# Taking weight loads out of the ends of the head groups of an attention-and-FFN backward kernel, and moving zero stores into them

## The chip, the cores and the metric

One core of one Trainium2 chip. The metric is the device time of one execution in microseconds (us), given as the median of the runs with the lowest and highest. "Span" is the same execution as the profiler sees it, some 1.8 us shorter than the time. "The median engine" of a store is the ninth of its sixteen landings.

## The reference

A decoder layer with attention over a window of a key-value cache and a gated FFN in parallel, forward and backward. Cut to what matters:

```python
# x 4x1x512; k_cache, v_cache 4x8x4096x128; wq 512x4096; wo 4096x512; FFN 512x1792; all bf16
def layer(x, k_cache, v_cache, wq, wo, w_gate, w_up, w_down):
    xn = layernorm(x)
    k, v = (repeat(c[:, :, 4096 - 1024:, :], 4, axis=1) for c in (k_cache, v_cache))   # the last 1024 of 4096
    o = softmax(q(xn @ wq) @ k.T / sqrt(128)) @ v
    return x + o @ wo + (gelu(xn @ w_gate) * (xn @ w_up)) @ w_down

out, vjp = jax.vjp(layer, ...)
return (out, *vjp(grad_out))          # the output and the gradients of x, both caches and all five weights
```

Two facts of it shape the kernel. The gradients of the two caches are as large as the caches (67 MB together), and three quarters of them are exact zeros, because only the last 1024 positions take part. Those zeros must still be written: 2 x 32 regions of 3072 x 128 bf16, 0.79 MB each, 50.3 MB of 112 MB moved in all.

## The kernel before

The eight key-value heads are worked through in NT = 4 groups of two heads (`GP = 2`). For each group the kernel loads slices of wo and wq (1 MB each) and blocks of both caches (`kb`, `vb`, 1 MB each), computes scores, softmax and its backward, and stores the gradients through staging buffers (`stg_dv`, `stg_dk`, `osb_o`, `osb_q`). SP issues these stores; GpSimd (POOL) issues the loads of the later groups; ACT issues the zero stores from one tile of zeros.

```python
    loads = deque()

    def load_w(t):
        eng = nc.gpsimd if t else nc.sync
        pool = wpool[t % 2]
        wo_t[t] = pool.tile([P, HG, D], BF16, name="wo_sb", tag="wo")
        eng.dma_start(out=wo_t[t][:], in_=wo_v[t])
        wq_t[t] = pool.tile([P, ND, CW], BF16, name="wq_sb", tag="wq")
        eng.dma_start(out=wq_t[t][:], in_=wq_v[t])
    ...
    def load_next(t):

        if t + 2 < NT:
            load_w(t + 2)
            for k in range(2):
                for g in range(GP):
                    loads.append(lambda k=k, g=g: load_kv(t + 2, k, g))
    ...
    def zeros(n):        # n regions, from one tile of zeros with ZP = 64 rows of 12 KB
        zs = ztile[0:P:P // ZP, :]
        while n > 0 and zruns:
            og, r = zruns[0]
            w = min(n, B * G - r, GP * 2)
            zsrc = bass.AP(tensor=zs.tensor, offset=zs.offset, ap=[list(zs.ap[0]), [0, w], [1, ZW]])
            zdst = og.rearrange("b g s d -> (b g) s d")[r:r + w, 0:K0, :].rearrange("r (m j) d -> m r (j d)", m=ZP)
            z = store(nc.scalar, zdst, zsrc, "zeros", ["rest", "zeros"])
            ...                     # ordered behind ACT's last evacuation
            n -= w
            ...
    def scores(t, k, hooks):        # k = 0 the keys, k = 1 the values
        for g in range(GP):
            for q in range(NQ):
                ...                 # transposes, evacuations and products of one K step
                if q == 1 and loads:
                    loads.popleft()()
                if q == 1:
                    zeros(ZN[t][GP * k + g])
    ...
        for t in range(NT):
            ...
            odq(t)
            fin(t)
            load_next(t)
            tick(len(bg))
            dw(t)
        tick(2)
        zeros(4)
        tick(len(bg))
        zeros(2 * B * G)            # whatever is left
```

Of the kernel before, what the change touches and what calls it, by code (L numbers as in the profile page):

```python
# [13 lines left out]
BF16 = mybir.dt.bfloat16  # L14
P = 128
# [3 lines left out]
def kernel(  # L19
# [29 lines left out]
    B, Sq, D = A_x.shape  # L49
# [7 lines left out]
    ND = D // P  # L57
# [4 lines left out]
    NT = G // GP  # L62
    HG = GP * rep
# [5 lines left out]
    CW = HG * Dh  # L69
# [46 lines left out]
    for c0 in range(0, NF, NF // 2):  # L116
        nc.sync.dma_start(out=wd_sb[:, c0:c0 + NF // 2, :],
                          in_=B_w_down[c0 * P:(c0 + NF // 2) * P, :].rearrange("(c p) n -> p c n", p=P))
# [47 lines left out]
    for b in range(B):  # L166
        nc.vector.tensor_copy(out=sel[:, :, b * rep:(b + 1) * rep],
                              in_=ident_f[:, b * RB:b * RB + 1].unsqueeze(2).broadcast_to([P, 2 * GP, rep]))
# [69 lines left out]
    for src, dstT, adj in ((dy_b, dyT, False), (xn_b, xnT, True)):  # L238
# [4 lines left out]
        if src is dy_b:  # L243
# [3 lines left out]
                                  in_=tps[:].rearrange("p c (b r) -> p c b r", b=B)[:, :, :, 0:8])  # L247
# [22 lines left out]
    wo_v = A_wo.rearrange("(t p k) n -> t p k n", p=P, k=HG)  # L270
    wq_v = A_wq.rearrange("(p c) (t j) -> t p c j", p=P, j=CW)
    wo_t, wq_t, k_t, v_t = {}, {}, {}, {}
# [3 lines left out]

    loads = deque()

    def load_w(t):
        eng = nc.gpsimd if t else nc.sync  # L280
        pool = wpool[t % 2]
        wo_t[t] = pool.tile([P, HG, D], BF16, name="wo_sb", tag="wo")
        eng.dma_start(out=wo_t[t][:], in_=wo_v[t])
        wq_t[t] = pool.tile([P, ND, CW], BF16, name="wq_sb", tag="wq")
        eng.dma_start(out=wq_t[t][:], in_=wq_v[t])

    def load_kv(t, k, g):
        d_, src, nm = ((k_t, A_k_cache, "kb"), (v_t, A_v_cache, "vb"))[k]
# [5 lines left out]
    def load_next(t):  # L294

        if t + 2 < NT:
            load_w(t + 2)
            for k in range(2):
                for g in range(GP):
                    loads.append(lambda k=k, g=g: load_kv(t + 2, k, g))  # L300
# [94 lines left out]
    def scores(t, k, hooks):  # L395

        lf = (qm, dom)[k]
        blks = (k_t, v_t)[k]
        ps = ps_a.tile([P, WQ], FP32, name="S_ps", tag=("S", "dP")[k])
        for g in range(GP):  # L400
            for q in range(NQ):
                T_ps = ps_w.tile([P, JQ, P], BF16, name="T_ps", tag="w")
                for jj in range(JQ):
                    nc.tensor.transpose(T_ps[:, jj, :], blks[(t, g)][:, q * JQ + jj, :], ident[:])  # L404
                T_sb = tsb.tile([P, WQ, B], BF16, name="T_sb", tag="T", bufs=4)
                evac(T_sb[:].rearrange("p n b -> p (n b)"), T_ps[:].rearrange("p j m -> p (j m)"), 1024, half=True)
                s = q * GP + g
                for b in range(B):
                    nc.tensor.matmul(ps[b * RG:(b + 1) * RG, :], lhsT=lf[:, b, s * RG:(s + 1) * RG],  # L409
                                     rhs=T_sb[:, :, b], start=(g == 0 and q == 0),  # L410
                                     stop=(g == GP - 1 and q == NQ - 1), tile_position=(0, b * RG))
                for f in hooks.get(g * NQ + q, ()):
                    f()
                tick(2 if k or q % 2 else 1)
                if q == 1 and loads:
                    loads.popleft()()
                if q == 1:
                    zeros(ZN[t][GP * k + g])
        st[t][("S", "dP")[k]] = ps[:]
# [90 lines left out]
    def odq(t):  # L510

        for j in range(J):
            for k in range(2):
                for g in range(GP):
                    pT, blks, r0 = st[t][("PT", "dST")[k]], (v_t, k_t)[k], (GP * k + g) * (P // 4)
                    nc.tensor.matmul(od_ps[r0:r0 + rep * B, 0, :], lhsT=pT[:, j % JQ, (j // JQ) * GP + g:P:NS],  # L516
                                     rhs=blks[(t, g)][:, j, :], start=(j == 0), stop=(j == J - 1),
                                     tile_position=(0, r0))
        rows = attw.tile([P, Dh], BF16, name="od_r", tag="od_r")
        nc.vector.tensor_scalar(out=rows[:], in0=od_ps[:, 0, :], scalar1=sc_od[:, 0:1], scalar2=None, op0=ALU.mult)  # L520
        T_ps = ps_w.tile([P, P], BF16, name="odT_ps", tag="w")
        nc.tensor.transpose(T_ps[:], rows[:], ident[:])
        dqT = attw.tile([P, GP, rep, B], BF16, name="od_T", tag="od_T")
        nc.vector.tensor_copy(out=dqT[:].rearrange("p g i b -> p g b i"),
                              in_=T_ps[:].rearrange("p (s x) -> p s x", s=2 * GP)[:, GP:2 * GP, 0:BI].rearrange(
                                  "p s (b i) -> p s b i", b=B))

        X = attw.tile([P, HG, Dh], BF16, name="od_x", tag="od_x", bufs=1)
        nc.gpsimd.tensor_tensor(out=X[:], in0=rows[:].unsqueeze(1).broadcast_to([P, HG, Dh]),
                                in1=hmsk[:].unsqueeze(2).broadcast_to([P, HG, Dh]), op=ALU.mult)  # L530
        st[t].update(dqT=dqT, X=X)
# [83 lines left out]


    NF4 = (NF + 3) // 4
    load_w(0)
    for k in range(2):
        for g in range(GP):  # L620
            load_kv(0, k, g)
# [141 lines left out]
    with tc.tile_pool(name="stage", bufs=4, reuse_waits="tile") as stage, \  # L763
            tc.tile_pool(name="wodd", bufs=1, reuse_waits="tile") as wodd:
        wpool.append(wodd)
        kvpool.append(wodd)
        load_w(1)
        for k in range(2):
            load_kv(1, k, 1)
        for t in range(NT):  # L770
            if t == 0:
                pre(t, {})
            masks(t)
            scores(t, 0, {})
            zeros(2 if t == 0 else 0)
            scores(t, 1, softmax(t))
            d1, d2 = softmax_d(t)
            zeros(4 if t == NT - 1 else 0)
            if t + 1 < NT:
                pre(t + 1, {0: [d1], 2: [d2]})  # L780
            else:
                tick(2)
                d1()
                tick(6)
                d2()
                tick(2)
            odq(t)
            fin(t)
            load_next(t)
            tick(len(bg))  # L790
            dw(t)
        tick(2)
        zeros(4)
        tick(len(bg))
        zeros(2 * B * G)


        acc_r = kvp.tile([P, 2, ND, B, RB], FP32, name="acc_r", tag="kb")
        nc.vector.tensor_copy(out=acc_r[:], in_=acc[:].unsqueeze(4).broadcast_to([P, 2, ND, B, RB]))
        fin_ps = []  # L800
        for o in range(2):
            f_ps = ps_w.tile([P, ND, P], FP32, name="f_ps", tag="w")
            for c in range(ND):
                nc.tensor.transpose(f_ps[:, c, :], acc_r[:, o, c].rearrange("p b r -> p (b r)"), ident_f[:])
            fin_ps.append(f_ps[:])
        acc_o, acc_d = fin_ps[0].rearrange("p c d -> p (c d)"), fin_ps[1].rearrange("p c d -> p d c")

        def adj(x):
            return x[:].rearrange("p (d c) -> p d c", c=ND)

        out_b = kvp.tile([P, D], BF16, name="out_b", tag="vb")
        nc.vector.tensor_tensor(out=out_b[:], in0=acc_o, in1=x_b[:], op=ALU.add)
        nc.sync.dma_start(out=out_0.rearrange("b s d -> (b s) d"), in_=out_b[0:P:RB, :])

        s1 = const.tile([P, 1], FP32, name="s1")
        nc.vector.reduce_sum(out=s1[:], in_=acc_d, axis=AX.XY)
        pr = kvp.tile([P, D], FP32, name="pr", tag="vb")
        s2 = const.tile([P, 1], FP32, name="s2")
        nc.vector.tensor_tensor_reduce(out=adj(pr), in0=acc_d, in1=adj(xn_f), scale=1.0, scalar=0.0,
                                       op0=ALU.mult, op1=ALU.add, accum_out=s2[:])  # L820
        nm1 = const.tile([P, 1], FP32, name="nm1")
        nc.vector.tensor_scalar(out=nm1[:], in0=s1[:], scalar1=-1.0 / D, scalar2=None, op0=ALU.mult)
        nm2 = const.tile([P, 1], FP32, name="nm2")
        nc.vector.tensor_scalar(out=nm2[:], in0=s2[:], scalar1=-1.0 / D, scalar2=None, op0=ALU.mult)
        nc.vector.scalar_tensor_tensor(out=adj(pr), in0=adj(xn_f), scalar=nm2[:, 0:1], in1=acc_d,
                                       op0=ALU.mult, op1=ALU.add)
        nc.vector.tensor_scalar(out=pr[:], in0=pr[:], scalar1=nm1[:, 0:1], scalar2=rstd[:, 0:1],
                                op0=ALU.add, op1=ALU.mult)
        dx_b = kvp.tile([P, D], BF16, name="dx_b", tag="kb")
        nc.vector.tensor_tensor(out=dx_b[:], in0=pr[:], in1=dy_b[:], op=ALU.add)  # L830
        nc.sync.dma_start(out=out_1.rearrange("b s d -> (b s) d"), in_=dx_b[0:P:RB, :])
# [30 lines left out]
```

## Time and profile before

| | before |
|---|---|
| time | 281.14 us (280.98 to 281.59, 3 runs) |
| span; mean granted TensorE clock | 279.9 us; 0.885 |
| PE, DVE, ACT, POOL busy | 77%, 57%, 41%, 20% |
| moved | 112.15 MB, 401 GB/s over the span |
| last compute | 269.1 us |
| last large store lands | 15 engines at 275.0 us, one at 278.8 us |

The last row is my reading of the semaphore updates in the trace: each large store has sixteen in this trace, and I take each as the landing of the part that one of the sixteen engines carries. The updates do not name the engines. The other rows are on the page. A page's slice view cuts the span into 40 equal slices, counted from 0 below. The stretch view gives a window, its length, then busy times with counts of instructions for PE, weight loads, DVE, ACT and POOL, then the clock, the mean busy share of the sixteen DMA engines, and GB/s.

### The profile page before, as it was taken

The numbers are of one execution on the slowest core, as the hardware profiler recorded it, in microseconds if no ns is written. First come the engines' busy times: TensorE is split into PE (matmuls) and PEld (weight loads), VectorE is DVE, ScalarE is ACT, GpSimd is POOL, SyncE is SP. The second block draws the span as 40 slices with busy tenths as digits, with TensorE's granted clock in tenths as the row PEclk, the third lists the DMA queues.
The fourth block names the chain that finished last, engine by engine and source line by source line (L and its number), as shares of the span: only waits on it lengthen the run. The fifth ranks groups of instructions, "written<-read, shape, count | busy, mean of one in ns | idle before, by whom it ended". The sixth has DMA issues, their size and how long they took to land.

```text
span 279.9 us, 7186 instructions
## 1 busy us (share of the span) xinstructions
PE 215.6 (77%) x3126; PEld 140.7 (50%) x3132; DVE 158.9 (57%) x336; ACT 115.3 (41%) x214; POOL 56.0 (20%) x56
## 2 busy tenths in 40 slices
PE   1868986978669869897799897778989769789700
PEld 0856864645346645454466654445665435255300
DVE  6955744645446655563657554547766444577740
ACT  1321733454335245543342553446245435714600
POOL 3890003230200334102001550010142020020000
PEclk9975979899986977997959979999999997898975
DMA  7999999999999999999999999999999999998992
GB/s 233 448 390 429 427 404 393 409 411 417 417 426 427 424 426 409 370 423 422 431 423 419 316 417 423 432 419 427 419 422 393 424 422 421 419 428 351 396 410 114
DMA packets 19440, 112.15 MB, mean 401 GB/s; under 512 B 1473, under 2 KB 5073, under 8 KB 10449
## 3 DMA queue, kind: packets, MB, share of 16 engines
q10 hardware_dynamic: 4416, 50.34, 42.8%
q1 hardware_dynamic: 12304, 44.58, 39.3%
q0 software_dynamic: 2688, 16.78, 15.4%
q8 instruction: 24, 0.39, 0.5%
q14 instruction: 8, 0.06, 0.1%
HBM read 30.68 MB, written 81.01 MB: 399 GB/s over the span
## 4 chain that ended last, share of the span: by engine, by line
PE 56%; DVE 21%; DMA 11%; issue 4%; ACT 2%; POOL 2%; ACTq 0%; DVEq 0%
PE kv_ps L544 11%; PE T_ps L404 9%; DVE T_sb L101 6%; PE S_ps L409 6%; DMA out_dram<-osb_d 6%; DMA out_dram<-osb_g 5%; PE dwo_ps L563 3%; PE acc_ps L213 3%; PE wgT_ps L749 3%; PE wqT_ps L602 3%; PE od_ps L516 3%; PE woT_ps L341 2%; POOL P_x L424 2%; PE pT_ps L435 2%; PE dwq_ps L575 2%
## 5 line engine op out<-in xcount | busy, mean ns | idle before, releaser
L101 DVE COPY T_sb<-T_ps 128x1024 bf16<-128x1024 bf16 x64 | 43.9, 690 | 44.6 <-PE T_ps L404 44.2
L99 ACT CAST stg_dv<-kv_ps 128x512 bf16<-128x512 f32 x57 | 30.4, 592 | 30.4 <-PE kv_ps L544 30.4
L99 ACT CAST stg_dk<-kv_ps 128x512 bf16<-128x512 f32 x40 | 22.2, 588 | 40.3 <-PE kv_ps L544 26.8
L544 PE MATMUL kv_ps<-domr,P_x 128*128 128x512 bf16 x63 | 23.4, 446 | 5.4 <-POOL P_x L424 4.8
L544 PE MATMUL kv_ps<-qmr,dS_x 128*128 128x512 bf16 x60 | 22.3, 459 | 1.8 <-DVE dS_x L424 1.4
L389 POOL TENSOR_TENSOR domr<-r,msk 128x512 bf16<-128x512 bf16 x8 | 8.2, 1040 | 75.1 <-DVE r L382 75.1
L404 PE MATMUL T_ps<-ident,kb 128*128 128x128 bf16 x256 | 22.0, 226 | 0.0
L404 PEld LDWEIGHTS <-kb 128*128 128x128 bf16 x256 | 17.3, 102 | 9.2 <-issue 6.7
L99 ACT CAST osb_g<-dwg_ps 128x512 bf16<-128x512 f32 (+1 forms) x28 | 14.3, 538 | 17.9 <-PE dwg_ps L722 8.0
L404 PE MATMUL T_ps<-ident,vb 128*128 128x128 bf16 x256 | 21.4, 227 | 0.1
L99 ACT CAST osb_o<-dwo_ps 128x512 bf16<-128x512 f32 x25 | 14.6, 586 | 15.3 <-PE dwo_ps L563 14.3
L404 PEld LDWEIGHTS <-vb 128*128 128x128 bf16 x256 | 16.5, 102 | 6.8 <-issue 4.7
L424 POOL TENSOR_TENSOR P_x<-P_b,bmsk 128x1024 bf16<-128x1024 bf16 x4 | 7.6, 1891 | 57.9 <-ACT P_b L472 57.9
L409 PE MATMUL S_ps<-T_sb,dom 128*32 128x256 bf16 x128 | 12.7, 387 | 8.0 <-DVE T_sb L101 7.5
L99 ACT CAST osb_q<-dwq_ps 128x512 bf16<-128x512 f32 x25 | 13.9, 590 | 9.6 <-PE dwq_ps L575 7.5
L101 DVE CAST stg_dk<-kv_ps 128x512 bf16<-128x512 f32 x24 | 16.1, 685 | 2.3 <-PE kv_ps L544 2.2
L409 PE MATMUL S_ps<-T_sb,qm 128*32 128x256 bf16 x128 | 13.1, 389 | 5.1 <-DVE T_sb L101 5.1
L101 DVE COPY woT<-woT_ps 128x1024 bf16<-128x1024 bf16 x16 | 11.0, 689 | 10.2 <-PE woT_ps L341 10.2
L101 DVE COPY wqT<-wqT_ps 128x1024 bf16<-128x1024 bf16 x16 | 11.0, 688 | 6.1 <-PE wqT_ps L602 6.1
L341 PE MATMUL woT_ps<-ident,wo_sb 128*128 128x128 bf16 x128 | 12.3, 249 | 2.7 <-DVE stg_dv L101 1.9
L341 PEld LDWEIGHTS <-wo_sb 128*128 128x128 bf16 x128 | 10.5, 114 | 7.1 <-issue 6.2
L409 PEld LDWEIGHTS <-dom 128*32 128x32 bf16 x128 | 5.3, 93 | 17.5 <-issue 15.7
(214 smaller groups left out, 404.8 us busy)
## 6 DMA issues: line engine op xcount, KB each, us to landing
out_dram<-ztile ACTq DMA_DIRECT2D x13, 3072.0 KB, 19.7
out_dram<-ztile ACTq DMA_DIRECT2D x6, 1536.0 KB, 18.9
out_dram<-stg_dv SPq DMA_DIRECT2D x8, 1024.0 KB, 19.8
out_dram<-stg_dk SPq DMA_DIRECT2D x8, 1024.0 KB, 12.2
kb<-in_A_k_cache_dram POOLq DMA_DIRECT2D x5, 1024.0 KB, 20.4
vb<-in_A_v_cache_dram POOLq DMA_DIRECT2D x5, 1024.0 KB, 25.6
out_dram<-osb_o SPq DMA_DIRECT2D x8, 512.0 KB, 14.5
out_dram<-osb_q SPq DMA_DIRECT2D x8, 512.0 KB, 13.6
```

The costliest lines, as they stand in the source:

```text
L99: last.append(nc.scalar.copy(out=out, in_=in_))
L101: return nc.vector.tensor_copy(out=out, in_=in_)
L213: nc.tensor.matmul(ps[:, c, :], lhsT=lf(c), rhs=rhs, start=(k == 0), stop=(k == len(terms) - 1))
L341: nc.tensor.transpose(wT_ps[:, i, c, :], wo_sb[:, 2 * h2 + i, c * P:(c + 1) * P], ident[:])
L404: nc.tensor.transpose(T_ps[:, jj, :], blks[(t, g)][:, q * JQ + jj, :], ident[:])
L409: nc.tensor.matmul(ps[b * RG:(b + 1) * RG, :], lhsT=lf[:, b, s * RG:(s + 1) * RG], rhs=T_sb[:, :, b], start=(g == 0 and q == 0), stop=(g = ...
L424: eng.tensor_tensor(out=dst[:].rearrange("p j (m b) -> p (j m) b", b=B), in0=src[:].unsqueeze(2).broadcast_to([P, WQ, B]), in1=bmsk[:].uns ...
L516: nc.tensor.matmul(od_ps[r0:r0 + rep * B, 0, :], lhsT=pT[:, j % JQ, (j // JQ) * GP + g:P:NS], rhs=blks[(t, g)][:, j, :], start=(j == 0), s ...
L544: nc.tensor.matmul(mps[:].rearrange("p q d -> p (q d)"), lhsT=src[:, jj, :], rhs=mr[:, g].rearrange("p q d -> p (q d)"), start=True, stop= ...
L563: nc.tensor.matmul(mps[:], lhsT=X[:].rearrange("p h d -> p (h d)")[:, g * rep + i:CW:HG], rhs=dyz[:], start=True, stop=True)
L602: nc.tensor.transpose(wT_ps[:, i, c, :], wq_sb[:, c, h * Dh:(h + 1) * Dh], ident[:])
L749: nc.tensor.transpose(wT_ps[:, i, c, :], wsb[:, c, fc * P:(fc + 1) * P], ident[:])
```

## The change

Its intent is to fill four hollows of the transfers, at the ends of the groups. At such an end the two weight loads and the first cache loads of a later group used to be issued together. Now the weights, too, wait in the queue of loads and go out one by one among the next group's K steps. In addition one zero region is stored at the end of groups 1 and 2, and two at the end of group 3; the call for four at the very end becomes one for two. No byte is added or taken away.

```diff
-    def load_w(t):
+    def load_w(t, k):
         eng = nc.gpsimd if t else nc.sync
         pool = wpool[t % 2]
-        wo_t[t] = ...; dma          wq_t[t] = ...; dma
+        if k == 0:  wo_t[t] = ...; dma
+        else:       wq_t[t] = ...; dma
 ...
         if t + 2 < NT:
-            load_w(t + 2)
+            for k in range(2):
+                loads.append(lambda k=k: load_w(t + 2, k))
             for k in range(2):
                 for g in range(GP):
                     loads.append(lambda k=k, g=g: load_kv(t + 2, k, g))
 ...
-                if q == 1 and loads:
+                if (q == 1 or (k, q) == (0, 3)) and loads:
                     loads.popleft()()
 ...
             odq(t)
+            zeros(2 if t == NT - 1 else min(t, 1))
             fin(t)
             load_next(t)
 ...
         tick(2)
-        zeros(4)
+        zeros(2)
         tick(len(bg))
         zeros(2 * B * G)
```

(The two lines with `...; dma` are shortened; the first loads of groups 0 and 1 are unchanged in effect.)

More of the change, by code (lines that the diff above doesn't have):

```diff
@@ L277 @@
     loads = deque()
-    def load_w(t):
+    def load_w(t, k):
         eng = nc.gpsimd if t else nc.sync
         pool = wpool[t % 2]
-        wo_t[t] = pool.tile([P, HG, D], BF16, name="wo_sb", tag="wo")
-        eng.dma_start(out=wo_t[t][:], in_=wo_v[t])
-        wq_t[t] = pool.tile([P, ND, CW], BF16, name="wq_sb", tag="wq")
-        eng.dma_start(out=wq_t[t][:], in_=wq_v[t])
+        if k == 0:
+            wo_t[t] = pool.tile([P, HG, D], BF16, name="wo_sb", tag="wo")
+            eng.dma_start(out=wo_t[t][:], in_=wo_v[t])
+        else:
+            wq_t[t] = pool.tile([P, ND, CW], BF16, name="wq_sb", tag="wq")
+            eng.dma_start(out=wq_t[t][:], in_=wq_v[t])
     def load_kv(t, k, g):
@@ L617 @@
     NF4 = (NF + 3) // 4
-    load_w(0)
+    for k in range(2):
+        load_w(0, k)
     for k in range(2):
@@ L766 @@
         kvpool.append(wodd)
-        load_w(1)
+        for k in range(2):
+            load_w(1, k)
         for k in range(2):
```

## The prediction

> **What bounds the kernel now.** I read the page's slice view first. Its lower lines give, for each fortieth of the span, the mean busy share of the 16 DMA engines in tenths, and what they moved.
>
> ```profile
> DMA  7999999999999999999999999999999999998992
> GB/s 233 448 390 429 427 404 393 409 411 417 417 426 427 424 426 409 370 423 422 431 423 419 316 417 423 432 419 427 419 422 393 424 422 421 419 428 351 396 410 114
> DMA packets 19440, 112.15 MB, mean 401 GB/s; under 512 B 1473, under 2 KB 5073, under 8 KB 10449
> ```
>
> The reader should see a row of nines: transfers run from the first microseconds to the end, near 424 GB/s, with hollows in slices 16, 22 and 36. PE is busy for 77%, but the DMA engines hardly rest. 112.15 MB at 424 GB/s alone take 264.5 us of the 279.9 us span. So the kernel is bound by its bytes, and a change that moves no byte away can win only what is lost between them.
>
> Next, the busy times by stretch, to size the hollows (columns: stretch and its length; PE, weight loads, DVE, ACT, POOL busy; then clock, DMA share, GB/s).
>
> ```profile
> 112.00:116.00 4.00, 3.58 (x40) 2.08 (x39) 2.47 (x5) 1.91 (x4) 1.30 (x3) 1.00 0.99 325
> 116.00:154.00 38.00, 31.59 (x453) 19.61 (x454) 21.39 (x42) 15.62 (x30) 3.21 (x3) 0.87 1.01 424
> 154.00:160.00 6.00, 4.98 (x72) 3.74 (x72) 3.69 (x7) 3.71 (x7) 3.69 (x4) 1.00 0.93 302
> 160.00:210.00 50.00, 42.57 (x668) 27.52 (x667) 29.52 (x58) 22.81 (x43) 10.19 (x10) 0.97 1.01 422
> 210.00:214.00 4.00, 4.00 (x53) 2.42 (x50) 2.26 (x5) 2.25 (x4) 2.04 (x2) 1.00 0.92 381
> ...
> 256.00:260.00 4.00, 3.92 (x20) 1.62 (x19) 3.29 (x6) 2.39 (x5) 0.00 (x0) 0.57 0.59 240
> 260.00:275.00 15.00, 4.11 (x19) 1.91 (x17) 7.61 (x15) 3.74 (x7) 0.00 (x0) 0.83 0.99 407
> 275.00:278.00 3.00, 0.00 (x0) 0.00 (x0) 0.00 (x0) 0.00 (x0) 0.00 (x0) 0.50 0.07 26
> ```
>
> The four hollows are the four group ends. Against 424 GB/s they lack 4 x (1 - 325/424) = 0.9 us, 6 x (1 - 302/424) = 1.7 us, 0.4 us and 1.7 us: 4.8 us together (estimate). This is what the change aims at.
>
> The last line decides my prediction. From 275 to 278 us the share is 0.07, which is one engine of sixteen (1/16 = 0.0625). The DMA queues of the hollow's end and of the tail show the same lone engine:
>
> ```profile
> DMA packets 35, 0.08 MB, mean 26 GB/s; under 512 B 2, under 2 KB 2, under 8 KB 35
> q1 hardware_dynamic: 35, 0.08, 6.6%
> ```
>
> That is 275 to 278 us. In the trace the semaphore updates of the last large store (osb_q, issued at 265.1 us) come from 15 engines at 274.9 to 275.0 us, and from one at 278.8 us. The stg_dk store issued at 252.4 us lands in the median engine at 257.7 us, in the last at 265.8 us. So through the hollow of 256 to 260 us, in which the others rest, this **one late engine** works on a backlog. I followed its packets backwards (the next starts 3 to 4 ns before the last one's end): from 43 us to 278.4 us I find no gap in it over 0.1 us. Its packets are the others' in number and size, but stretched by some 11 us in total more than normal lengths (12 KB: usually 0.460 us).
>
> Compute is not the end: the chain of waits ends its work with dx_b at 269.1 us. The list of waits has no wait of PE for a load, and late in the kernel one 0.2 us wait for a store's buffer.
>
> [...]
>
> **The change, part by part.** I compared the order of both programs' instructions.
>
> *Weights.* Groups 2 and 3 still load 1 MB of wo and 1 MB of wq each; POOL still spends 0.53 and 0.76 us to issue them. For group 2 only wq moves: behind the two qmr products (2.04 us), so from 106.9 to some 112 us. It is needed at about 149 us (dq_ps), and lands in 17.6 to 27.0 us: hidden. For group 3, od_x goes ahead of the two domr products (2.04 us), wq ahead of wo, and kb behind them. kb moves from 157.1 to about 165 us, is needed past 210 us and lands within 31 us: hidden. At two group ends X is ready some 2 us earlier; PE has other work there (4.98 us of 6 busy), so perhaps 0.5 us of the compute chain, which isn't the end.
>
> In the hollows at 112 and 154 us the software queue runs nearly alone (81% and, at 156 to 160 us, 84% of the engines), with slow packets: the sum over the normal length is 12.8 us at 110 to 115 us and 20 us at 155 to 160 us, over sixteen engines 0.8 and 1.25 us. Breaking up the run of loads and adding a store should remove most of this.
>
> *Zero regions.* One is 64 x 12,288 B = 0.79 MB, 1.9 us at 424 GB/s. The 3.1 MB issued at 258.3 us go; one region is issued near 149 us, one near 199 us, two near 249 us (ahead of group 3's stores). The number is 64 before and after. Two more issues on ACT's queue, 0.61 us each, lie in its idle time (ACT 41% busy). The semaphores they wait for belong to transfers 10 us and more landed, so ACT shouldn't stall.
>
> *Sum, if all engines were alike.* The hollows fill: at 154 us 1.9 us of zeros meet 1.7 us of lack, at 256 us 3.7 us meet 1.7. Some 3 to 4.5 us of 4.8 come back, the end goes from 281.1 to about 277.
>
> *Sum for the late engine.* Its bytes are the same: zero. It had no gap in the hollows. It can win only the slow software packets, some 1.8 us in all between 43 and 278 us for it, of which I let a third to a half go: 0.6 to 0.9 us. So 281.1 - 0.8 = **280.3 us**. The fifteen others then end near 271 to 272 us, and the lone tail grows from 3.8 to about 6 us.
>
> **Rivals.**
> *A: the hollows are time* (277 us, or 276.3 at the very best: 281.1 - 4.8). For it: the hollows are there, and extra work is put exactly into them. Against it: the lone engine's backlog in each of them and the 3 us tail at 26 GB/s. It would be right if the late engine isn't the same one in all hollows, so that it rested at 154 us; my following of packets could have swapped engines there.
> *B: compute becomes the end, or waits for buffers.* More zeros ahead of stg_dk and osb stores make them land up to 3.7 us later (1.57 MB at 424 GB/s), and four buffers each of stg and osb are reused. For it: the 20 to 29 us from issue to landing of osb_q. Against it: waits of this kind are 0.2 us late in the kernel, and the compute end has 9 us of room before 278.8 us. I expect no more than 0.5 us.
> *C: later loads are late.* kb of group 3 goes last in a burst of four loads. It would make PE wait at about 210 us; there are some 45 us from issue to use. Cost nil; if real, 1 to 3 us.
>
> **Range and chances.** Late engine, 70%: 279.6 to 281.3. Rival A in part or whole, 22%: 276.5 to 279.5. B, C or more stretched packets on the late engine, 8%: 281.5 to 283. Hence 280.3, with 278.3 to 281.7 eight times in ten. The 2% line is at 275.5, below even the 4.8 us ceiling: 2% for faster. Slower would need 286.8: 1%.
>
> **What would show it.** In the slices of the changed kernel, slices 22 and 36 should be filled to about 400 or more GB/s (right for both sums). Right for mine: a longer stretch at the end with a share of 0.06 to 0.07 and 26 GB/s, while the others stop at about 272 us. Wrong: the share falls from 0.9 to nothing within a microsecond, at about 273 us. Rival B would show as waits of ACT or DVE for out_dram stores after 160 us, C as waits of PE for kb or vb. The compute end should stay at 268 to 269 us.

What it took from the trace stands elsewhere: one engine ends 3.8 us after fifteen, alone it moves 26 GB/s at 275 to 278 us, and with all engines busy the total is 424 GB/s (116 to 154 us). The sum stays 281.1 - 0.8 = 280.3 us.

## The result and the profile after

The time after is 281.12 us (280.63 to 281.61, 6 runs), before 281.11 us (280.98 to 281.59, 6 runs). The ratio is 0.9999, 95% interval 0.9986 to 1.0012: no difference. A ratio here is the mean time of one kernel's fast runs over the mean of the other's in the same rounds, so it is not quite the ratio of the medians that are quoted. The output is correct.

The slices of the kernel after, to be read against those that the prediction shows:

```profile
span 279.4 us, 7193 instructions
...
DMA  7999999999999999999999999999999999999970
GB/s 236 447 389 430 425 403 420 406 419 427 420 425 424 427 417 393 409 400 416 415 424 427 381 412 425 426 424 423 424 420 424 426 424 422 425 428 421 424 308 20
DMA packets 19471, 112.15 MB, mean 401 GB/s; under 512 B 1504, under 2 KB 5104, under 8 KB 10480
```

The hollows are nearly filled: slice 16 went from 370 to 409 GB/s, slice 22 from 316 to 381, slice 36 from 351 to 421. What was won stands at the far end. The last two slices fell from 410 and 114 to 308 and 20: the work ran out earlier, and the end stayed where it was. The same by stretches:

```profile
112.00:116.00 4.00, 3.50 (x40) 2.07 (x39) 2.52 (x4) 1.83 (x4) 2.00 (x4) 1.00 1.01 416
154.00:160.00 6.00, 4.52 (x87) 3.58 (x87) 2.95 (x6) 3.06 (x6) 3.50 (x4) 1.00 1.01 375
...
210.00:214.00 4.00, 4.00 (x66) 2.56 (x64) 2.22 (x5) 2.24 (x4) 2.04 (x2) 1.00 1.01 420
256.00:260.00 4.00, 4.00 (x14) 1.49 (x12) 3.51 (x7) 2.83 (x5) 0.00 (x0) 0.57 1.00 418
260.00:270.00 10.00, 3.77 (x18) 1.84 (x16) 7.29 (x14) 3.49 (x7) 0.00 (x0) 0.83 0.99 409
270.00:272.00 2.00, 0.00 (x0) 0.00 (x0) 0.00 (x0) 0.00 (x0) 0.00 (x0) 0.50 0.45 176
272.00:275.00 3.00, 0.00 (x0) 0.00 (x0) 0.00 (x0) 0.00 (x0) 0.00 (x0) 0.50 0.06 27
275.00:278.00 3.00, 0.00 (x0) 0.00 (x0) 0.00 (x0) 0.00 (x0) 0.00 (x0) 0.50 0.06 26
```

The second stretch moves 375 GB/s where it moved 302, the fourth in this list 418 where it moved 240. Only this last one had been mainly a rest of engines, with a share of 0.59 before. At 112 and 154 us the share was 0.99 and 0.93 before: the engines were busy there, with the slow packets of the software queue (summed over the sixteen engines, 12.8 us over their normal length at 110 to 115 us and 20.0 us at 155 to 160 us). Then look at the share just before the end: 0.99, 0.45, 0.06, 0.06. From 272 us on one engine of sixteen works alone at 26 GB/s. Before, this lone stretch was 3.8 us long; now it is 5.9 us. The queues of 275 to 278 us in the kernel after confirm that this is one queue with 37 packets:

```profile
DMA packets 37, 0.08 MB, mean 26 GB/s; under 512 B 2, under 2 KB 2, under 8 KB 37
...
q1 hardware_dynamic: 37, 0.08, 6.6%
```

The loads themselves moved little. By POOL's issues, wq of group 2 went from 106.9 to 112.1 us. For group 3, wq went from 161.2 to 157.7, wo from 160.7 to 163.0, and one kb from 157.1 to 163.5 us.

The landings say it store by store. This is my reading of the semaphore updates in the trace (us; issue, median engine, last but one, last):

```
kernel   store    issued   median   last but one   last
before   stg_dk   252.43   257.7    260.0          265.8
before   osb_q    265.13   275.0    275.0          278.8
after    stg_dk   251.97   263.8    265.1          271.0
after    osb_q    266.61   271.3    272.5          278.4
after    out_b    268.61   270.4    270.8          271.1   (4 rows)
after    dx_b     269.33   270.9    271.0          271.3   (4 rows)
```

Fifteen engines finish 2.5 us sooner than before, the sixteenth at the same time (278.4 against 278.8, with a span that is 0.5 us shorter in this profile). Compute ends at 267.75 us, 1.3 us sooner; that does not matter either.

Of the waits of the kernel after for a transfer, the list of waits names these, by engine, tile and line, with sum, count and longest in us:

```profile
ACT osb_g L99 <- DMA out_dram<-osb_d: 5.1, 2, 4.0
ACT osb_g L99 <- DMA out_dram<-osb_g: 2.7, 1, 2.7
ACT stg_dv L99 <- DMA out_dram<-osb_q: 0.8, 1, 0.8
```

The first two belong to the FFN's stores early in the kernel, before any of the changed places. The third is at 238 to 239 us; it is a wait of 0.8 us for a store's buffer, of the kind that the prediction names under rival B. The full list has one more, of 0.8 us for wd_sb at the very start. No engine waits for a load that the change moved.

### The profile page after: what moved, and what is told of

Read it like the earlier page. It is cut to its first block, busy times and chain, and to the rows that moved or that the text cites. A ratio compares the mean times of both kernels' runs of the same rounds, so it can differ in the third digit from the quotient of the medians.

```text
span 279.4 us, 7193 instructions
## 1 busy us (share of the span) xinstructions
PE 212.5 (76%) x3132; PEld 138.1 (49%) x3132; DVE 159.9 (57%) x336; ACT 115.3 (41%) x214; POOL 56.1 (20%) x56
## 3 DMA queue, kind: packets, MB, share of 16 engines
q10 hardware_dynamic: 4448, 50.34, 42.9%
## 4 chain that ended last, share of the span: by engine, by line
PE 48%; DVE 19%; DMA 15%; issue 9%; POOL 3%; ACT 2%; DVEq 0%; POOLq 0%; ACTq 0%; SPq 0%
PE kv_ps L547 9%; PE T_ps L407 8%; DMA out_dram<-osb_d 6%; DMA out_dram<-osb_q 6%; DVE T_sb L101 5%; PE S_ps L412 5%; DMA out_dram<-ztile 4%; PE acc_ps L213 3%; PE od_ps L519 3%; PE dwo_ps L566 3%; PE wqT_ps L605 2%; PE woT_ps L344 2%; PE wgT_ps L753 1%; POOL P_x L427 1%; PE dwg_ps L726 1%
## 5 line engine op out<-in xcount | busy, mean ns | idle before, releaser
L407 PEld LDWEIGHTS <-kb 128*128 128x128 bf16 x256 | 17.9, 104 | 10.7 <-issue 8.3
L407 PE MATMUL T_ps<-ident,kb 128*128 128x128 bf16 x256 | 22.7, 231 | 0.0
L532 POOL TENSOR_TENSOR od_x<-od_r,hmsk 128x1024 bf16<-128x1024 bf16 x4 | 7.6, 1901 | 36.7 <-DVE od_r L523 36.7
L605 PEld LDWEIGHTS <-wq_sb 128*128 128x128 bf16 x128 | 9.1, 104 | 10.4 <-issue 8.9
L605 PE MATMUL wqT_ps<-ident,wq_sb 128*128 128x128 bf16 x128 | 11.0, 230 | 3.9 <-issue 3.3
```

The lines of the kernel that those rows point to most:

```text
L407: nc.tensor.transpose(T_ps[:, jj, :], blks[(t, g)][:, q * JQ + jj, :], ident[:])
L532: nc.gpsimd.tensor_tensor(out=X[:], in0=rows[:].unsqueeze(1).broadcast_to([P, HG, Dh]), in1=hmsk[:].unsqueeze(2).broadcast_to([P, HG, Dh]) ...
L605: nc.tensor.transpose(wT_ps[:, i, c, :], wq_sb[:, c, h * Dh:(h + 1) * Dh], ident[:])
```

## The experiments

Twelve kernels ran, each beside the kernel before on the same chip (281.2 to 281.4 us there). Four kernels had slow executions: runs 3 and 6 two of six each, runs 4 and 5 one of six. The medians below take them in, the ratios do not.

| run | time, us | ratio to before (95%) |
|---|---|---|
| 1 loads only | 281.22 (281.13 to 281.96) | 1.0008 (0.9988 to 1.0027) |
| 2 zero regions only | 281.15 (280.78 to 281.54) | 0.9999 (0.9978 to 1.0020) |
| 3, 4 one engine left out of four regions, in after and before | 283.06, 283.17 | 1.0050, 1.0067 |
| 5, 6 region in seven, eight parts at the end of group 1 | 295.88, 295.78 | 1.0506, 1.0483 |
| 7 two regions left out | 277.60 (277.34 to 278.56) | 0.9880 (0.9861 to 0.9899) |
| 8 region in six parts, group 3 | 285.12 (284.20 to 286.18) | 1.0144 (1.0120 to 1.0169) |
| 9 in eight parts | 284.75 (284.31 to 285.74) | 1.0132 (1.0110 to 1.0155) |
| 10 in four parts | 284.06 (283.81 to 284.42) | 1.0092 (1.0072 to 1.0112) |
| 11 in four parts, zero move only | 283.73 (283.37 to 284.07) | 1.0075 (1.0053 to 1.0098) |
| 12 in five parts | 286.37 (284.94 to 287.08) | 1.0167 (1.0132 to 1.0202) |

My theory was that of the prediction: one late engine has a backlog of its own, so only fewer bytes on that engine move the end. The rivals: the hollows are time, and some new wait eats the gain; or the two halves of the change cancel, one winning and one losing.

### 1 and 2: each half alone

```diff
  (run 1: the change without its zero move)
-            zeros(2 if t == NT - 1 else min(t, 1))
-        zeros(2)
+        zeros(4)
  (run 2: the kernel before with the zero move alone)
+            zeros(2 if t == NT - 1 else min(t, 1))
-        zeros(4)
+        zeros(2)
```

> The weight loads spread over the next group's K steps, the zero regions as before. Late-engine theory (one of the 16 DMA engines works without a pause and ends 4 to 6 us after the others, so only its own work sets the end): 281.1, within 0.7 us; the lone tail at 26 GB/s stays. Theory that the hollows are time: the hollows at 112 and 154 us fill by 1 to 1.5 us, so 279.6 to 280.2.

> The zero regions moved as in the change, the loads as before. Late-engine theory: 281.1, within 0.7 us; the other fifteen engines stop at about 272 to 273 us, the last one at 278 to 279. Theory that the hollows are time: 277.5 to 278.5. Theory of two effects that cancel (spread loads win, earlier zeros lose, or the reverse): this run and the loads-only run lie on opposite sides of 281.1, each by over 1 us.

Neither half moves the time. The halves are not quite clean, since the order of the instructions is made anew for every program: POOL issues group 3's loads in run 1 in the order of the kernel before (kb, wo, wq after the first vb), in run 2 in that of the kernel after (wq, wo, kb), although the loads are written as before there. The stretches of the kernel with the loads only:

```profile
112.00:116.00 4.00, 3.22 (x35) 1.78 (x33) 2.06 (x3) 1.76 (x3) 1.01 (x2) 1.00 1.00 419
154.00:160.00 6.00, 5.71 (x100) 4.61 (x98) 3.17 (x8) 2.36 (x5) 1.60 (x2) 0.74 1.00 392
...
275.00:278.00 3.00, 0.00 (x0) 0.00 (x0) 0.00 (x0) 0.00 (x0) 0.00 (x0) 0.50 0.06 25
```

And of the kernel with the zero regions only:

```profile
154.00:160.00 6.00, 5.71 (x109) 4.31 (x107) 4.08 (x9) 3.26 (x7) 3.26 (x4) 1.00 1.01 411
256.00:260.00 4.00, 3.15 (x11) 1.19 (x10) 3.22 (x6) 2.49 (x5) 0.00 (x0) 1.00 0.99 421
260.00:270.00 10.00, 2.29 (x9) 1.69 (x8) 4.62 (x10) 1.66 (x3) 0.00 (x0) 0.60 0.92 379
270.00:272.00 2.00, 0.00 (x0) 0.00 (x0) 0.23 (x1) 0.00 (x0) 0.00 (x0) 0.50 0.17 67
...
275.00:278.00 3.00, 0.00 (x0) 0.00 (x0) 0.00 (x0) 0.00 (x0) 0.00 (x0) 0.50 0.06 25
```

Each alone already fills hollows (392 and 411 GB/s where 302 stood), and each ends with the same lone engine. With the zero move alone the share is down to 0.17 after 270 us, and fifteen engines have landed their part of the last large store by 271.2 us, 7 us ahead of the sixteenth. So the halves do not cancel; neither does anything to the end.

### 7: fewer bytes on every engine

Two regions at the ends of groups 1 and 2 are never written; the result is wrong there. A region is 64 packets of 12 KB (4096 for the 64 regions in the trace), on average 4 for each of the sixteen engines, of 0.46 us each.

```diff
-            zeros(2 if t == NT - 1 else min(t, 1))
+            zeros(2 if t == NT - 1 else 0)
+            if t in (1, 2):
+                zruns[0][1] += 1        # skip one region
```

> The changed kernel without the two zero regions at the ends of groups 1 and 2 (never written, so a wrong result on purpose): 1.57 MB less, 8 packets of 0.46 us less for each engine. Late-engine theory: 3.7 us less, 277.4, with a lone tail of the same length that only comes earlier. Theory that the compute end (dx_b at about 268 us) and a fixed landing after it set the time: 281.1.

277.60 us: the expected 277.4 within the scatter. (POOL issues group 3's loads here in the order of run 1.) The end moved with the bytes, 8 packets x 0.46 = 3.7 us of them, although nothing in compute was touched. The profile keeps the same shape with an earlier end:

```profile
270.00:272.00 2.00, 0.00 (x0) 0.00 (x0) 0.00 (x0) 0.00 (x0) 0.00 (x0) 0.50 0.07 27
...
275.00:278.00 3.00, 0.00 (x0) 0.00 (x0) 0.00 (x0) 0.00 (x0) 0.00 (x0) 0.54 0.00 0
```

The lone engine stands at 270 to 272 us already, and at 275 us nothing moves; its last landing is at 274.7 us where it was at 278.4. This is what the filled hollows did not do. Alone it would fit any bound by bytes, since the engines carry less on average; together with runs 1 and 2, where fifteen engines ended sooner for nothing, it supports the theory.

### 3 and 4: relieving one engine

If the end is one engine's backlog, taking work from that engine should beat both kernels. I did not know which one it is. The first try was to leave one out. Four regions were written as 60 rows, meant for fifteen engines, and the rest in 12 short rows, meant for twelve. The page of run 3 fits these two numbers: its queue 10 has 54 packets more than that of the kernel after (4502 against 4448). The rows of the cut stores account for 32 of them. Two stores on fifteen engines and two on twelve, in place of two on sixteen, would give the other 22 at one small packet for each engine of a store; between the kernels before and after, two whole stores more made just 32 (4416 to 4448). Which engine is left out no trace shows.

```diff
+            else:                       # four regions in groups 1 and 2
+                zstore(0, 60, ZP, ZW)
+                zstore(180, 192, 192, ZW // 3)
```

> The changed kernel, with four of the 64 zero regions cut so that 60 of their 64 rows go over 15 engines (four rows each, as before) and the last four rows over 12. The bytes are the same. [...] Late-engine theory[...]: it ends at about 271, the others at 272 to 273, the kernel at 275 to 276.5, and the lone tail is gone. [...] Theory that total bytes or the compute end set the time: 281.1.

> The kernel before, with the same four zero regions[...]. Late-engine theory[...]: now the fifteen others set the end, at 275.0 to 275.6 us of the span instead of 278.8, so 277 to 278; the change would then be worth the 2 to 3 us by which its fifteen end earlier. If it is another engine: 281 to 282, and the change is worth nothing here either. Theory that total bytes or the compute end set the time: 281.1.

The times that stand there after "Late-engine theory" hold if the engine that is left out is the late one: it then has 16 packets of 0.46 us, 7.4 us, less, and the twelve engines of the short rows 0.6 us more (estimates from the length of the packets). If the late one was among those twelve, the first expected 281.5 to 282 us, and if among the other three of the fifteen, 281.

Both were slower, by 0.50% (0.24 to 0.77) and 0.67% (0.24 to 1.1), with a wide scatter. In both profiles, which fell on the fastest execution of each kernel, the last landing of the last large store was at 278.8 and 278.9 us, as before. But the other engines came much later than without the cut: last but one at 278.6 in place of 272.5 us, and 277.5 in place of 275.0, where packets alone explain 0.6 us. The trace shows where part of this arose: between 190 and 210 us, when cut stores ran, the 12 KB zero packets took 23.7 and 17.9 us more than their usual length, summed over the engines, and 2.1 us in each of the two kernels without the cut. What stretched them stays open. So these runs give no sign that the engine left out is the late one, but they alone do not exclude it; runs 8 to 12 do better.

### 5 and 6: a failed pair

Next a region at the end of group 1 was split so that only seven, or eight, engines carry it. That such a store runs on as many engines as it has parts is my reading of the updates: in the runs from 8 on, a store of 4, 5, 6 and 8 parts shows 5, 6, 7 and 9 of them, one some 1.7 to 1.8 us after the issue, which I leave out, and one for each part. The small stores of four rows look the same: out_b in the kernel before, issued at 265.9 us, has one update at 267.5 us and four at 275.1 to 275.2 us. For seven parts I have no count. Which engines these are, no view names.

```diff
+            elif part == 7:
+                zstore(rows[:, 0:3024, :].rearrange("r (m i j) d -> m (r i) (j d)", m=7, i=9), ...)
+                zstore(rows[:, 3024:3072, :].rearrange("r (m j) d -> m r (j d)", m=16), ...)
-            zeros(2 if t == NT - 1 else min(t, 1))
+            zeros(2 if t == NT - 1 else min(t, 1), part=7 if t == 1 else None)
```

> The changed kernel, with one of the 64 zero regions (the one at the end of group 1) cut into 7 parts of 9 rows, so that 7 DMA engines carry 9 packets of 0.46 us each and the other nine none, where all 16 carried 4. Bytes are the same. Late-engine theory: if the late engine is none of the seven, it has 1.8 us less and ends at about 276.6; the seven have 2.3 us more and end near 274.9: 279.3. If it is one of the seven: 283.4. Theory that total bytes or the compute end set the time: 281.1.

> The same with 8 parts of 8 rows: eight engines carry 8 packets each. Late-engine theory: if the late engine is none of the eight, 279.3; if it is one of them, 1.8 us more: 283. [...]

Both took 295 to 296 us, far beyond either expectation, and tell nothing of the late engine. The changed program came out in another order: POOL issued wo last of six loads, at 162.35 us in place of 162.97 as third, and it landed at 209 us in place of 179. PE waited for it, as the list of waits of the seven-part run says:

```profile
PE woT_ps L355 <- DMA wo_sb<-in_A_wo_dram: 18.9, 1, 18.9
```

The stretch beside it has the transfers at little more than half:

```profile
200.00:220.00 20.00, 10.52 (x181) 6.77 (x182) 7.54 (x13) 5.26 (x10) 0.00 (x0) 0.68 0.57 240
```

This looks like the prediction's rival C made real by accident: the order of the later loads can matter, at some 14 us, and the change under study just keeps it harmless. The cut store itself was not run apart from that order here, but the cut stores of runs 8 to 12 cost 2 to 5 us and not 14.

### 8 and 9: which engines the late one is among

One of the two regions at the end of the last group, in six or eight parts; the order on PE, POOL, DVE and SP is that of the kernel after.

```diff
+            elif part == 6:
+                zstore(rows.rearrange("r (m i j) d -> m (r i) (j d)", m=6, i=16), [[18 * ps, 6], [0, 16], [1, 4096]])
-            zeros(2 if t == NT - 1 else min(t, 1))
+            zeros(1 if t == NT - 1 else min(t, 1))
+            if t == NT - 1:
+                zeros(1, part=6)
```

> The two runs before this were spoiled by a new order of loads; here the order on every engine but one more store on ACT is that of the changed kernel. Of the two zero regions at the end of the last group, one is cut into 6 parts, so that six engines carry 16 packets of 8 KB (16 x 0.309 = 4.9 us) and ten carry none, where all 16 carried 4 of 12 KB (1.8 us). Late-engine theory: if the late engine is none of the six, it ends 1.8 us earlier, near 276.6, the six near 275.6 by then: 279.3. If it is one of the six, 3.1 us later: 284.2. Theory that total bytes or the compute end set the time: 281.1.

> The same with 8 parts: eight engines carry 8 packets of 12 KB (3.7 us), eight none. Late-engine theory: if the late engine is none of the eight, 279.3; if it is one, 283.0. [...] Theory that total bytes or the compute end set the time: 281.1 in both.

Both became slower, and in both the lone engine ended later, at 282.0 and 282.1 us in place of 278.4. The six-part run:

```profile
272.00:275.00 3.00, 0.00 (x0) 0.00 (x0) 0.00 (x0) 0.00 (x0) 0.00 (x0) 0.50 0.55 216
275.00:278.00 3.00, 0.00 (x0) 0.00 (x0) 0.00 (x0) 0.00 (x0) 0.00 (x0) 0.50 0.06 26
278.00:280.00 2.00, 0.00 (x0) 0.00 (x0) 0.00 (x0) 0.00 (x0) 0.00 (x0) 0.50 0.06 26
```

I took it from this that the late engine carries parts in both. With six parts it would get 16 packets of 8 KB (0.31 us) in place of 4 of 12 KB: +3.1 us expected, +3.6 measured. With eight it would get 8 packets of 12 KB: +1.8 expected, and +3.6 measured. The second number does not fit packets alone; in that run the lone engine was later than in the kernel after even before the change's place (osb_o, issued near 219 us, landed at 247.2 in place of 243.0 us, and the store of eight parts was issued at 247.7).

### 10, 11 and 12: four parts and five

If the late engine carries none of the four parts, a region in four parts takes 1.8 us from it (4 packets of 0.46 us). The small last stores of four rows, out_b and dx_b, spoke for that: they landed everywhere by 271.3 us, while the late engine still had 7 us of packets to move. That these stores and one of four parts use the same four engines was my assumption; no trace shows it.

```diff
+            elif part == 4:
+                zstore(rows.rearrange("r (m i j) d -> m (r i) (j d)", m=4, i=16), [[18 * ps, 4], [0, 16], [1, 6144]])
+                zeros(1, part=4)          # run 10 in the kernel after, run 11 in that of run 2
+            elif part == 5:               # run 12; 72 of 3072 rows of the region stay unwritten, on purpose
+                zstore(rows[:, 0:3000, :].rearrange("r (m i j) d -> m (r i) (j d)", m=5, i=15),
+                       [[18 * ps, 5], [0, 15], [1, 5120]])
```

> The kernel after with one of the two regions at the end of the last group written in four parts (16 packets of 12 KB each) in place of 64 parts. A store of four rows is carried by four engines; such an engine gets 16 x 0.46 = 7.4 us of packets in place of 1.8 us, every other engine 1.8 us less. In the runs with six and with eight parts the one late engine got later by 3.6 us[...]. Theory[...]: the late engine ends 1.8 us sooner (276.6 us of its span), the four end at 271.5 + 5.5 = 277, so a time of 279.3 to 280.0 us, ratio 0.993 to 0.996. Rival (it is among the four): 281.1 + 5.5 = 286.6 us or more, ratio 1.02. Second rival (splitting the store in two costs of itself, as the 1.8 us above the packets in the run with eight parts may say): 281.5 to 283 us, with the lone engine ending at 278.5 to 280 us.

> The same four-part region in the kernel with the zero move alone, where the fifteen others stopped at 270.3 us: the four end at about 275.8 us, and the late engine, relieved of 1.8 us, at 276.6 us. Theory (late engine not among the four): 279.3 us, ratio 0.993, a time below both kernels. Rival (it is): 286.6 us, 1.02. If splitting the store costs of itself: 281 to 283 us in both this run and the one on the kernel after.

> The kernel after with that region in five parts of 15 packets of 10 KB (the last 72 rows of the region are not written: wrong on purpose in that corner). An engine among the five gets about 15 x 0.385 = 5.8 us in place of 1.8, the others 1.8 us less. [...] If the four-part run is slow too, this one tells nothing of its place.

The theory of run 10 is that the late engine carries none of the four parts. The sums of run 12 were 279.3 us (ratio 0.993) if it carries none of the five, and 281.1 + 3.9 = 285.0 us (1.014) if it carries one.

Neither four-part run is the faster kernel that the theory promised, nor as slow as its rival said: 284.06 and 283.73 us, between the two, and a little above the second rival's 281.5 to 283. The five-part run is wrong in the unwritten corner and slower still.

The landings tell the engines apart. My reading of the updates of the last large store, osb_q (us; the five latest of sixteen):

```
run                     the five latest landings
10 four parts           274.0   274.4   277.2   277.6   281.3
12 five parts           275.0   275.0   275.0   275.1   282.3
```

In run 10 four engines are behind the rest, which stand at 273.9 us, and a fifth one is later still: the late engine is none of the four. In the trace of run 12 it is visibly one of the five, because only it still has 8 KB packets after 268.6 us, and between them are the 10 KB packets of the five-part store (queue 10 is ACT's, queue 1 SP's):

```
run 12, packets of one engine, us          run 10, packets of the late engine, us
269.09-269.40  q1   8192                   268.49-269.11  q1  8192
269.40-269.78  q10 10240                   269.12-269.71  q1  8192
269.78-270.09  q1   8192                   269.72-270.32  q1  8192
270.08-270.47  q10 10240                   270.32-270.87  q1  8192
270.47-270.78  q1   8192                   270.87-271.25  q1  8192
270.77-271.33  q10 10240                   271.25-271.55  q1  8192
271.33-271.64  q1   8192                   271.55-271.86  q1  8192
```

Run 12's lone engine ends 3.9 us after that of the kernel after (282.3 against 278.4), and 15 x 0.385 - 1.84 = 3.9 us is what such an engine gains in packets. That the two agree so well is partly luck: in this run the late engine was 0.7 us ahead before (242.3 against 243.0 us for the same osb_o), and the profiled execution is the fastest of its kernel, 1.4 us below the median. By these readings the store of five parts includes it, and that of four does not. For six and eight parts only the later end speaks, and run 10, just below, has an engine without parts that ends later too. Which of the sixteen it is, no view names.

Then why was run 10 not faster? The right-hand column shows it. There the late engine carries no zeros at all, and yet its 8 KB packets take 0.6 us each up to 271.25 us, and 0.31 from then on. The last packets of the four-part store end within 0.15 us of that moment, at 271.14 us. From 260.1 to 271.25 us I count a row of 19 such packets; at 0.31 us each they would have taken 5.9 us, so 5.3 us were lost. The landings agree: the late engine needed 4.7 us for its eight packets of the second stg_dv store (266.5 to 271.2), in the kernel after 2.5 us (266.1 to 268.5). Sum: 1.8 us won, 5.3 lost, so +3.5 us; its end moved by +2.8 (281.3 against 278.4). From 243 us on, 29 of 495 packets of 8 KB on queue 1 took over 1.15 times the usual length in run 10, none of 512 in the kernel after. The ends in the stretch view of run 10:

```profile
275.00:278.00 3.00, 0.00 (x0) 0.00 (x0) 0.00 (x0) 0.00 (x0) 0.00 (x0) 0.50 0.15 60
278.00:280.00 2.00, 0.00 (x0) 0.00 (x0) 0.00 (x0) 0.00 (x0) 0.00 (x0) 0.50 0.07 26
```

Here 0.15 is more than one engine: the four loaded ones finish within this stretch, and then the lone one goes on alone as ever.

What halves the rate is not shown. My part-wise stores read their zeros from rows of the tile that lie 18 partitions apart (0, 18, 36, 54 for four parts), the whole stores from every second one; whether that matters no run tells. The trace of run 10 shows a second engine without parts that was slowed. Of the stg_dk store issued at 258.7 us, ten engines land by 264.4 us, the four with parts from 268.9 us on, the late one at 276.2 us, and one without parts at 266.5 us; run 11 shows the same (267.3 us). The five-part run, which takes rows 18 partitions apart as well, does not show as large a loss. A version to try next would take the zeros of the four parts from other rows of the tile. If nothing slowed it, the late engine would gain 1.8 us and the time would be an estimated 279.3 us (281.1 - 1.8), 0.7% below both kernels. It was not run.

### What stays open

No correct version of mine beats the two kernels. Why one engine is late at all is not settled. As I followed its packets, they are the others' in size, and are stretched, above all those of the zero stores between 210 and 260 us (in the kernel before, the 12 KB packets that start then take 5.4 us more than 0.46 us each, summed over all engines); no run found what stretches them. One candidate was left out of the account. Queue 8, which the profile's page calls instruction and counts into the share of the sixteen engines, moves 24 packets of 16 KB, of 0.88 to 1.36 us each, 22.8 us in sum before and 22.4 after. In the kernel after, within 25 ns of the end of each of the 24, one packet of another queue starts that takes 0.28 to 0.50 us longer than usual (12 KB: 0.82 to 0.87 in place of 0.46 us), 9.7 us in sum. How these fall on the engines no view tells, and no run moved them. At some 0.93 + 0.4 us each, four or five more of them on one engine than on the others would make a lag of 6 us (an estimate from these figures). That the late engine never rests before 200 us rests on following packets backwards, which can swap engines: by landings its lag in the kernel before is 0.4 us at 214 us, 3.0 us at 229 us and 5.8 us at 266 us.

## Why the prediction was right

The time, 281.1 us, is within the range of 278.3 to 281.7 and 0.8 us above the number; the outcome is the one given 97%.

- **Bound by bytes.** Right. Two regions less gave -3.5 us in the median where the bytes give -3.7 (run 7), while 2.5 us less for fifteen engines and 1.3 us less for compute gave nothing.
- **The four hollows get filled.** Right, nearly in full: 416, 375, 420 and 418 GB/s. Slice 22 reached 381 and not the 400 that I asked for; the stretch at 154 to 160 us still lacks a tenth.
- **The hollows are no time (against rival A).** Right. Both halves of the change alone fill them and leave the end alone (runs 1 and 2). The others stop at about 272 us and the lone tail grows to 5.9 us, as predicted (6).
- **Slow packets of the software queue, 0.6 to 0.9 us.** This is the term that failed in size. The slow packets did become fewer: what they took beyond their normal length fell from 48.7 to 22.0 us, summed over the sixteen engines. The time fell by nothing (0.9999, at most 0.14% by the interval, 0.4 us). That the late engine has its share of these was an assumption; it evidently has not, or gets it back elsewhere. The whole of the 0.8 us by which the number lay under the time before rests on this term, so the time is in the range because the rest of the sum is zero, not because of this term.
- **Rival B.** Right to give it little: after 160 us the kernel after has one wait for a store's buffer, of 0.8 us (0.2 before). Run 2 had three of 4.5 to 5.8 us and took the same time. Compute ended at 267.75 us, slightly before the predicted 268 to 269.
- **Rival C.** Right for this change: the later loads land in time. Runs 5 and 6 show that the guard is thin, since in another order of the same loads PE waited 18.9 us for wo (run 5) and the time was 14 us longer.
- **The late engine is the same one throughout.** Supported for the end: runs 10 and 12 fit one engine that carries none of four parts and one of five (last landings at 281.3 and 282.3 us). For the first 200 us it is not shown, and the lag grew mostly after 210 us. A rest of the late engine in the hollow at 154 us should have shown as a gain, and there was none. Two readings of the prediction are stronger than its lines. Its second fence shows the queues of the tail only, not of the hollow's end. And the others did not all rest from 256 to 260 us: the share there is 0.59, and the last but one engine lands its stg_dk at 260.0 us.

## What to carry to other kernels

A hollow in what the DMA engines move was worth nothing, because, as I read the landings, the engine that ends last did not rest in it (shown for the one at 256 to 260 us: its part of stg_dk landed at 265.8 us, the median at 257.7 us). So look first at how many engines are busy in the last microseconds (a share of 0.06 is one of sixteen) and at how far the last landing of a store lies behind the median. Here one engine was late: evening out the schedule for the other fifteen won nothing (0.9999), and 1.57 MB less won 3.5 us at once (run 7). A store that was spread over fewer engines to relieve a late one took more than it gave here (run 10: 5.3 us lost, 1.8 us won): compare the length of the packets of the other queues, and the order of the loads, before believing in the count of bytes.
